# The last outer product of a two-level fast matrix product: how its held output stores are issued, and its last chunk in halves

## The chip, the cores and the metric

The kernel runs on one core of a Trainium2 chip. The metric is the device time of one execution in microseconds (us). A core has five instruction streams that matter here: TensorE (PE; its weight loads are listed apart as PEld), VectorE (DVE), ScalarE (ACT), GpSimd (POOL) and SyncE (SP). Each runs its own instructions in order, and they wait for one another through semaphores. SP and ACT can issue DMAs; before the change only SP issues the ones spoken of here.

## What is computed

An attention block feeds a two-layer block. In short, with 8 batches, 12 heads, 448 tokens and head dimension 64 (all in float32):

```python
q_n, k_n = rmsnorm(q, g_q), rmsnorm(k, g_k)
attn = softmax(q_n @ k_n.T / sqrt(64))
x = (attn @ v)            # to (8 * 448, 768)
h = x @ w_in              # w_in: 768 x 2048
out = (h - tanh(h)) @ w_out   # w_out: 2048 x 768
```

## The kernel before

The attention of later batches runs interleaved with the two layers of earlier ones. The layers are done by a seven-product scheme: a 2 x 2 block product is made of seven smaller products of sums and differences of blocks, named 1 to 7 and run in the order `ORDER = (1, 5, 6, 2, 3, 7, 4)`. The products 2, 3 and 7 accumulate into the PSUM banks of 1, 5 and 6. There are three banks for this (`mm_162`, `mm_163`, `mm_164` in the program, all "mm" in the profile).

For batches 2 to 7 the second layer is done for two batches at once, by `project_pair`, and the scheme is used twice. Outside are seven outer products in the order `OUTER = (1, 2, 3, 7, 6, 5, 4)`, whose 2 x 2 blocks are the two halves of the hidden units, the two batches, and the halves of the output columns. Each outer product makes three chunks of 128 output columns for 448 tokens (`m` = 0, 1, 2; `HC` is 3, `CD` is 6). Chunks 0 and 1 come out of seven inner products of 224 tokens, each four contractions long; the third chunk comes out of a plain product of 448 tokens and eight contractions. In the profile each float32 matmul shows as two records, so an inner product is 8 records and the third chunk 16.

After each inner product's matmuls (L1094) `flush()` runs what was put off in `late["todo"]` and one step of `late["calm"]` (two in some places of outer product 4). Then the bank is read: product 1 is copied by ScalarE to `s1` (L1168), product 2 is copied by ScalarE (L1174), the others are added by VectorE (`add`, L1101). When a chunk is whole, `combine_outer` adds it into what the pair's chunks need; the chunks that are held across outer products lie in the tiles `acc` and `acc2`. For third chunks the adds are made at once, else they go on the list `late["calm"]` as well, as do the stores.

`store(b, n, y, o)` turns a finished chunk of 128 columns by 448 tokens on VectorE in 32 x 32 blocks (L950) into another tile, and puts off the issue of its four DMAs (L955) on the list `late["out"]`. `step_out()` counts those entries down and issues them; it is called before each product's matmuls, so a store goes to SP's queue one product after its transpose stands in the program. Each of the four DMAs writes 32 partitions of 14 runs of 128 bytes to the output, 448 runs and 56 KB. All go out on SP, behind each other and behind the loads of weights into the ring `w_f` (`ring_load`), which SP issues too. Tiles that await a store are named th, th_more, s and acc.

The program is written as a fixed order per engine (`manual_schedule`): nothing is rearranged, and the order of the calls in the Python code is the order of each engine's instructions. The last outer product is number 4 for batches 6 and 7. After it, `mlp` runs the remaining `todo` and `calm` work and issues what is left in `late["out"]`. The kernel then branches over a second, general path to the closing instructions (L1797).

Of the kernel before, what the change touches and what calls it, by code (L numbers as in the profile page):

```python
# [146 lines left out]
def bounded_path(tc, ctx, q, k, v, moe_w_in, moe_w_out, out, g_col, ident, ones, half_ones, neg_half, early):  # L147
# [66 lines left out]
    def mm_bank():  # L214
        return bank_of("mm")
# [649 lines left out]
    def hidden(b):  # L865
# [74 lines left out]

        return products(b, 0, SETS, 2, HC, moving, done_with)

    def store(b, n, y, o=None):

        if o is None:
            o = part("th").rearrange("p f s -> p (f s)")
        nc.vector.transpose(out=o, in_=y if b >= FIRST else y.rearrange("r (c p) -> r p c", c=NCH))  # L950

        def issue():
            for i in range(P // BL):
                d = n * P + i * BL
                nc.sync.dma_start(  # L955
                    out=out[b * S : (b + 1) * S, d : d + BL].rearrange("(j t) d -> t j d", t=BL),
                    in_=o[i * BL : (i + 1) * BL].rearrange("t (j d) -> t j d", d=BL),
                )

        late["out"].append([1 if b >= PAIRED else 2, issue])  # L960

    def step_out(by=1):
        for entry in late["out"]:
            entry[0] -= by
        while late["out"] and late["out"][0][0] <= 0:
            late["out"].pop(0)[1]()

    def calm_step(twice=False):
        for _ in range(1 + twice):
            if late["calm"]:  # L970
                late["calm"].pop(0)()
# [93 lines left out]
    def project_pair(b, ks):  # L1065

        if ks[0] == 0:
            late["acc"] = [late["pair"].tile([P, HC, S], F32, name=name) for name in ("acc", "acc2")]
        acc, acc2 = late["acc"]
        us = late["us"]  # L1070
        low, high = slice(0, HS), slice(HS, S)
        outer_plan = {
            3: {1: (0, SETS - 1), 5: (1, SETS - 1)},
            7: {1: (2, 0), 5: (2, 1), 6: (2, 2), 2: (2, 3)},
            6: {1: (3, 0), 6: (3, 1), 3: (3, 2), 4: (3, 3)},
        }
        inner_plan = {5: 0, 6: 1, 7: 2, 4: 3}
        inner_at = {6: 0, 3: 1, 7: 2, 4: 3}
        calm = late["calm"]

        def at(k, q):

            p = OUTER[k]
            if q in outer_plan.get(p, {}):
                outer_sum(*outer_plan[p][q])
            if k == SOON and q == 1:
                inner_sum(p, 2)
                inner_sum(p, 3)
            if q in inner_at and k + 1 in ks:
                inner_sum(OUTER[k + 1], inner_at[q])  # L1090

        def matmuls(bank, n, w, moving, first):
            for i, mv in enumerate(moving):
                nc.tensor.matmul(  # L1094
                    bank[:, :n], lhsT=w(i), rhs=mv, start=(first and i == 0), stop=(i == len(moving) - 1),
                    skip_group_check=not first,
                )
                yield 4 * n / ENGINE_NS

        def add(out, x, y, op=ALU.add):  # L1100
            nc.vector.tensor_tensor(out=out, in0=x, in1=y, op=op)  # L1101

        def combine_outer(p, m, y):

            e, f = acc[:, m], acc2[:, m]
            if p in (1, 3):
                if m == HC - 1:
                    nc.scalar.copy(out=e if p == 1 else f, in_=y)
                return
            third = m == HC - 1  # L1110
            o = y
            if third and p in (2, 5, 4):
                o = f if p == 2 else e if p == 4 else part("s1").rearrange("p f s -> p (f s)")

            def soon(*args):
                if third:
                    add(*args)
                else:
                    calm.append(lambda: add(*args))

            if p == 2:
                soon(o, y, e)
                calm.append(lambda: store(b, m, o))
            elif p == 7:
                soon(e, e, y)
                soon(f, f, y, ALU.subtract)
            elif p == 6:
                soon(e, e, y)
            elif p == 5:
                soon(o, y, e)  # L1130
                calm.append(lambda: add(f, f, o))
                calm.append(lambda: store(b + 1, HC + m, o))
                calm.append(lambda: store(b + 1, m, f, o))
            else:
                soon(o, y, e)
                calm.append(lambda: store(b, HC + m, o, f if third else e))

        def flush():
            now, late["todo"] = late["todo"], []
            for fn in now:  # L1140
                fn()
            calm_step(p == 4 and q in (3, 7, 4))

        for k in ks:
            p = OUTER[k]
            step = ring_steps.index((b, 2, p, 1))
            if p in (1, 3):
                y1, y2 = ((acc if p == 1 else acc2)[:, m] for m in range(2))
            else:
                y1, y2 = (part(n).rearrange("p f s -> p (f s)") for n in ("s2", "s5"))  # L1150
            s1 = part("s1").rearrange("p f s -> p (f s)")
            banks = {}
            for i, q in enumerate(ORDER):
                ring_load(step + 5 + i // 2)
                step_out()
                w = ring_tiles[b, 2, p, 1 + i // 2][:, i % 2 * HB : (i % 2 + 1) * HB].rearrange("p (f d) -> p f d", d=P)
                first = q not in (2, 3, 7)
                bank = banks[q] = mm_bank() if first else banks[{2: 1, 3: 5, 7: 6}[q]]
                if q in (1, 2, 3):
                    moving = [rows(p, KB * (q > 1) + c, 1, high if q == 3 else low)[:, 0] for c in range(KB)]  # L1160
                else:
                    u = us.pop((p, inner_plan[q])) if q != 5 and q != 6 else us[p, inner_plan[q]]
                    moving = [u[:, c] for c in range(KB)]
                yield from matmuls(bank, HS, lambda c: w[:, c], moving, first)
                flush()
                v = bank[:, :HS]
                if q == 1:
                    nc.scalar.copy(out=s1[:, low], in_=v)  # L1168
                elif q == 5:
                    add(y2[:, low], v, s1[:, low])  # L1170
                elif q == 6:
                    add(y1[:, high], v, s1[:, low])
                elif q == 2:
                    nc.scalar.copy(out=y1[:, low], in_=v)  # L1174
                elif q == 7:
                    add(y2[:, high], v, y2[:, low])
                    add(s1[:, low], v, s1[:, low])
                elif q == 3:
                    add(y1[:, high], v, y1[:, high])
                    late["todo"].append(lambda p=p, y=y1: combine_outer(p, 0, y))  # L1180
                elif q == 4:
                    add(y2[:, low], v, s1[:, low])
                    late["todo"].append(lambda p=p, y=y2: combine_outer(p, 1, y))
                at(k, q)
            ring_load(step + 9)
            step_out()
            w = ring_tiles[b, 2, p, 0].rearrange("p (f d) -> p f d", d=P)
            bank = mm_bank()
            yield from matmuls(bank, S, lambda i: w[:, i], [rows(p, f, 1, slice(0, S))[:, 0] for f in range(HF)], True)
            flush()  # L1190
            late["todo"].append(lambda p=p, v=bank[:, :S]: combine_outer(p, HC - 1, v))

# [79 lines left out]

    def mlp():
        late["todo"], late["keep"], late["inner"], late["calm"], late["out"] = [], [], None, [], []
        for b in range(PAIRED):
            yield from hidden(b)
            yield from project(b) if b else project_first(b)
        for fn in late["todo"]:
            fn()
        late["todo"] = []  # L1280
        single_stack.close()
        late["pair"] = pool("pair", bufs=1)
        for b in range(PAIRED, B, 2):
            yield from hidden(b)
            while late["inner"] is not None:
                inner_step()
            yield from project_pair(b, range(SOON))
            yield from hidden(b + 1)
            yield from project_pair(b, range(SOON, len(OUTER)))
        for fn in late["todo"]:  # L1290
            fn()
        while late["calm"]:
            calm_step()
            step_out()
        step_out(2)
# [506 lines left out]
```

## Time and profile before

| What | Value |
|---|---|
| Median of three runs | 1356.81 us (1356.78 to 1357.18) |
| The profiled execution's own time | 1356.19 us |
| Its span, first to last instruction | 1354.4 us |
| TensorE busy | 1317.9 us, 97% of the span |
| VectorE, ScalarE, GpSimd busy | 949.1, 556.9 and 775.1 us |
| Last matmul ends | 1343.9 us |
| Last transpose on VectorE ends | 1345.2 us |
| First and last of the output stores that SP issues after 1328 us | 1328.5 and 1349.7 us |

The span is measured from the first to the last instruction on the core. The time of the execution is 1.8 us more. Times of single instructions are counted from the start of the span. A DMA's row shows how long the issuing engine was occupied with it; the landing of its data is listed apart.

### The profile page before, as it was taken

What the parts mean: (1) busy time and instruction counts of PE and PEld (TensorE: products, weight loads), DVE (VectorE), ACT (ScalarE), POOL (GpSimd) and SP (SyncE); (2) the same over time, 40 slices, a digit from 0 to 9 for tenths busy, and PEclk for the clock granted to TensorE, in tenths of its full rate; (3) what the DMA queues carried; (4) which work ended last, traced back from release to release, by engine and by line L of the source; (5) the groups of instructions that cost most, each with busy time, mean ns of one, the idle gap of its engine ahead of it and who ended that gap; (6) DMA issues with size and microseconds to landing.
All of it is one profiled execution on the core that took longest, in us unless ns stands there. A gap on an engine that the chain in (4) does not pass through costs nothing.

```text
span 1354.4 us, 29206 instructions
## 1 busy us (share of the span) xinstructions
PE 1317.9 (97%) x11336; PEld 1029.0 (76%) x11336; DVE 949.1 (70%) x1393; ACT 556.9 (41%) x1326; POOL 775.1 (57%) x591
## 2 busy tenths in 40 slices
PE   7989999999999999999999999999999999999996
PEld 3467854478998878697778787778787888699985
DVE  4999978757855768587887576768786668434453
ACT  7856654344433454445322446354512264311100
POOL 4766766347846256626698235844699253712761
PEclk9999999999999999999999999999999999999999
DMA  7879889889999667476655867476645775365544
GB/s 172 197 198 266 254 256 254 249 247 280 335 302 274 169 157 182 107 192 151 162 145 138 197 169 179 110 180 163 168 139 139 160 194 158 107 163 178 171 143 84
DMA packets 371688, 253.54 MB, mean 187 GB/s; under 512 B 282196, under 2 KB 310228, under 8 KB 371540
## 3 DMA queue, kind: packets, MB, share of 16 engines
q1 hardware_dynamic: 371536, 251.57, 68.9%
q8 instruction: 92, 1.51, 0.5%
q14 instruction: 56, 0.46, 0.1%
q10 hardware_dynamic: 4, 0.00, 0.0%
HBM read 205.23 MB, written 46.27 MB: 186 GB/s over the span
## 4 chain that ended last, share of the span: by engine, by line
PE 84%; DVE 9%; DMA 2%; SPq 2%; issue 1%; ACT 1%; POOL 1%; DVEq 0%; ACTq 0%
PE mm L841 36%; PE mm L1094 23%; PE sc L569 9%; PE sc L635 6%; PE mm L1258 5%; DVE xT L762 1%; PE sc L673 1%; PE sc L623 1%; SPq L955 1%; PE mm L673 1%; DVE rows L613 1%; DMA w_f<-w_in 1%; DVE rows L606 1%; DVE rows L600 1%; DMA w_f<-w_inner 0%
## 5 line engine op out<-in xcount | busy, mean ns | idle before, releaser
L841 PE MATMUL mm<-xT,w_f 128*128 128x224 f32 x1296 | 264.0, 353 | 0.7 <-DVE s L912 0.7
L841 PEld LDWEIGHTS mm<-xT,w_f 128*128 128x128 f32 x1296 | 244.5, 190 | 6.4 <-issue 4.8
L569 PE MATMUL sc<-qT,kT 64*32 64x448 f32 (+1 forms) x3072 | 214.2, 499 | 2.9 <-ACT p_last L575 1.7
L841 PE MATMUL mm<-tt,w_f 128*128 128x224 f32 x1044 | 213.7, 356 | 0.8 <-DMA w_f<-w_in 0.2
L841 PEld LDWEIGHTS mm<-tt,w_f 128*128 128x128 f32 x1044 | 194.9, 190 | 19.1 <-issue 15.4
L523 POOL TENSOR_TENSOR rr_mine<-rr_mine,neg_half 128x28 f32<-128x28 f32 x33 | 160.6, 4868 | 2.7
L758 DVE TENSOR_TENSOR xT<-xT,sc 128x448 f32<-128x448 f32 x32 | 19.9, 622 | 176.8 <-PE sc L569 119.3
L889 POOL TENSOR_TENSOR gT<-s,th 128x448 f32<-128x448 f32 x44 | 56.1, 1277 | 145.3 <-ACT th L888 142.0
L1094 PE MATMUL mm<-u,w_f 128*128 128x224 f32 x672 | 136.5, 354 | 1.2 <-DVE sum_all L733 0.9
L1094 PE MATMUL mm<-gT,w_f 128*128 128x224 f32 (+1 forms) x480 | 133.0, 429 | 3.1 <-DVE acc L1101 3.0
L1094 PEld LDWEIGHTS mm<-u,w_f 128*128 128x128 f32 x672 | 126.1, 190 | 8.2 <-POOL u L1051 3.9
L569 PEld LDWEIGHTS sc<-qT,kT 64*32 64x32 f32 x3072 | 71.0, 106 | 70.4 <-issue 50.5
L1094 PEld LDWEIGHTS mm<-gT,w_f 128*128 128x128 f32 x480 | 90.2, 190 | 40.7 <-issue 34.2
L635 PE MATMUL sc<-p,v_nat 64*32 64x448 f32 x1120 | 110.5, 536 | 0.0
L1094 PE MATMUL mm<-g,w_f 128*128 128x224 f32 (+1 forms) x360 | 99.5, 428 | 1.1 <-DVE acc L1101 1.1
L725 ACT COPY sum_g<-sum 32x14 f32<-32x14 f32 x280 | 56.3, 201 | 106.1 <-DVE sum L717 100.3
L889 POOL TENSOR_TENSOR g<-s,th 128x448 f32<-128x448 f32 x24 | 30.6, 1278 | 108.2 <-ACT th L888 93.3
L575 ACT ACTIVATE p<-sc 128x448 f32<-128x448 f32 x132 | 71.7, 543 | 50.3 <-PE sc L569 42.4
L1094 PEld LDWEIGHTS mm<-g,w_f 128*128 128x128 f32 x360 | 67.9, 190 | 28.2 <-issue 26.2
L1258 PE MATMUL mm<-gT,w_out 128*128 128x448 f32 x192 | 74.4, 543 | 0.0
L1051 POOL TENSOR_TENSOR u<-gT 128x448 f32<-128x448 f32 x48 | 58.8, 1247 | 11.1 <-PE mm L1094 11.1
L144 POOL TENSOR_TENSOR rr<-rr,neg_half 112x8 f32<-112x8 f32 (+1 forms) x30 | 49.4, 1675 | 26.7 <-DVE rr L143 26.2
(196 smaller groups left out, 2427.9 us busy)
## 6 DMA issues: line engine op xcount, KB each, us to landing
w_f<-w_in SPq DMA_DIRECT2D x196, 384.0 KB, 3.5
w_f<-w_inner SPq DMA_DIRECT2D x63, 512.0 KB, 3.7
w_f<-w_out SPq DMA_DIRECT2D x42, 512.0 KB, 3.9
w_raw<-in_moe_w_out_dram SPq DMA_DIRECT2D x16, 768.0 KB, 5.6
w_in<-w_out SPq DMA_DIRECT2D x21, 384.0 KB, 5.1
qk_nat<-in_q_dram SPq DMA_DIRECT2D x132, 56.0 KB, 2.8
qk_nat<-in_k_dram SPq DMA_DIRECT2D x132, 56.0 KB, 2.3
g<-w_out SPq DMA_DIRECT2D x14, 512.0 KB, 5.1
```

Source lines behind the costliest of these rows:

```text
L144: nc.gpsimd.tensor_tensor(out=r, in0=r, in1=neg_half[:rows], op=ALU.pow)
L523: nc.gpsimd.tensor_tensor(out=mine, in0=mine, in1=neg_half[:, :1].to_broadcast([P, 2 * NJ]), op=ALU.pow)
L569: nc.tensor.matmul(tiles[h][i * BL : (i + 1) * BL, :n], lhsT=kT[r, c * P + at : c * P + at + BL], rhs=qT[r, first : first + n], start=True ...
L575: nc.scalar.activation(p[:, h, c if c < 2 else 0, :], tiles[h][:, :n], AF.Exp, scale=1.0 if rr is None else rr[:, 0, 2 * c + h : 2 * c + h ...
L635: nc.tensor.matmul(av[g][i * BL : (i + 1) * BL, :S], lhsT=v_nat[keys, h, c, m * BL : (m + 1) * BL], rhs=p[keys, h], start=first, stop=True ...
L673: nc.tensor.matmul(av[n][r : r + BL, :HS], lhsT=v_nat[:, h, c, m * BL : (m + 1) * BL], rhs=p[c][:, h, n * HS : (n + 1) * HS], start=False, ...
L725: nc.scalar.copy(out=acc[h * BL : (h + 1) * BL, g], in_=part[g * BL : (g + 1) * BL, h * NJ : (h + 1) * NJ])
L841: nc.tensor.matmul(bank[:, f * HS : (f + 1) * HS], lhsT=w[:, c * width + f, :], rhs=moving[p](c), start=(first and f == 0 and c == 0), sto ...
L889: eng.tensor_tensor(out=g[:, rows, cols], in0=h, in1=th, op=ALU.subtract)
L1051: nc.gpsimd.tensor_tensor(out=u[:, half], in0=a[:, half], in1=z[:, half], op=ALU.subtract)
L1094: nc.tensor.matmul(bank[:, :n], lhsT=w(i), rhs=mv, start=(first and i == 0), stop=(i == len(moving) - 1), skip_group_check=not first,)
L1258: nc.tensor.matmul(bank[:, :S], lhsT=w_out_row(f, n // HC)[:, n % HC * P : (n % HC + 1) * P], rhs=g[:, f, :], start=(f == 0), stop=(f == C ...
```

## The change

There is a new flag, `late["ending"]`, which is set for the last outer product (number 4 of batches 6 and 7) only. With it set:

- In `flush()` all of the list `late["calm"]` is run at once, at the first inner product, and not one step at each.
- `store` issues its DMAs at once, after anything still held in `late["out"]` (`step_out(9)`), and the odd ones of the four go to ScalarE's queue and not SP's.
- Chunks 0 and 1 of this outer product's own result are added, turned and stored by the new `store_now`, two DMAs on SP and two on ScalarE.
- The third chunk is made in two halves of 224 tokens, each with its own bank, its own add, transpose and four DMAs of 32 partitions of 7 runs.

```diff
+    def store_now(b, n, y, o, cols):
+        nc.vector.transpose(out=o[:, cols], in_=y[:, cols])
+        for i in range(P // BL):
+            d = n * P + i * BL
+            (nc.sync, nc.scalar)[i % 2].dma_start(
+                out=out[b * S + cols.start : b * S + cols.stop, d : d + BL].rearrange("(j t) d -> t j d", t=BL),
+                in_=o[i * BL : (i + 1) * BL, cols].rearrange("t (j d) -> t j d", d=BL),
+            )
...
     def store(b, n, y, o=None):
...
         def issue():
             for i in range(P // BL):
                 d = n * P + i * BL
-                nc.sync.dma_start(
+                (nc.scalar if late["ending"] and i % 2 else nc.sync).dma_start(
...
+        if late["ending"]:
+            step_out(9)
+            issue()
+            return
         late["out"].append([1 if b >= PAIRED else 2, issue])
...
     def combine_outer(p, m, y):
...
+            if p == 4 and late["ending"]:
+                add(y, y, e)
+                store_now(b, HC + m, y, e, slice(0, S))
+                return
...
     def flush():
...
             calm_step(p == 4 and q in (3, 7, 4))
+            while late["ending"] and late["calm"]:
+                calm_step()

         for k in ks:
             p = OUTER[k]
+            late["ending"] = b + 2 == B and k == len(OUTER) - 1
...
             w = ring_tiles[b, 2, p, 0].rearrange("p (f d) -> p f d", d=P)
+            if late["ending"]:
+                y, o = acc[:, HC - 1], acc2[:, HC - 1]
+                for cols in (low, high):
+                    bank = mm_bank()
+                    moving = [rows(p, f, 1, cols)[:, 0] for f in range(HF)]
+                    yield from matmuls(bank, HS, lambda i: w[:, i], moving, True)
+                    flush()
+                    add(y[:, cols], bank[:, :HS], y[:, cols])
+                    store_now(b, CD - 1, y, o, cols)
+                continue
             bank = mm_bank()
```

More of the change, by code (lines that the diff above doesn't have):

```diff
@@ L1274, in mlp @@
         late["todo"], late["keep"], late["inner"], late["calm"], late["out"] = [], [], None, [], []
+        late["ending"] = False
         for b in range(PAIRED):
```

## The prediction, made before the changed kernel ran

> **What bounds the kernel now.** I read the page first, then only its last 30 us, since the diff acts nowhere else: the chain of waits by line, the end of the timeline, the tile that goes out (out_dram), and the instructions of the closing line.
>
> ```profile
> PE 1317.9 (97%) x11336; PEld 1029.0 (76%) x11336; DVE 949.1 (70%) x1393; ACT 556.9 (41%) x1326; POOL 775.1 (57%) x591
> ...
> PE 84%; DVE 9%; DMA 2%; SPq 2%; issue 1%; ACT 1%; POOL 1%; DVEq 0%; ACTq 0%
> ```
>
> TensorE is the bound up to its last matmul; after that SP's queue is (the SPq share of the chain). TensorE in the last outer product, from the timeline (columns: start, us, engine, line, op, tiles, shape, count):
>
> ```profile
> 1328.61 3.19 PE L1094 MATMUL mm<-u,w_f 128*128 128x224 f32 x16
> 1331.64 3.19 PE L1094 MATMUL mm<-gT,w_f 128*128 128x224 f32 x16
> 1334.66 3.19 PE L1094 MATMUL mm<-u,w_f 128*128 128x224 f32 x16
> 1337.69 6.18 PE L1094 MATMUL mm<-gT,w_f 128*128 128x448 f32 x16
> ...
> 1343.90 0.63 DVE L1101 TENSOR_TENSOR acc<-mm,acc 128x448 f32<-128x448 f32 x1 [4.01 <-PE mm L1094]
> 1344.57 0.65 DVE L950 STREAM_TRANSPOSE acc<-acc 128x448 f32<-128x448 f32 x1
> ```
>
> Each x16 is two inner products; product 1 ends just before the first row, the rows are 5 and 6, 2 and 3, 7 and 4, then the third chunk. It runs without a pause to 1343.87; the last data is transposed at 1345.22. SP's stores come later:
>
> ```profile
> 1347.57 0.43 SPq L955 DMA_DIRECT2D out_dram<-acc  x1
> 1349.70 0.32 SPq L955 DMA_DIRECT2D out_dram<-acc  x1
> L955 SPq DMA_DIRECT2D out_dram<-acc x12: 316/486/1073, 1342.6 to 1349.7; - x12
> DMA to landing us min/median/max: 1.7/2.7/4.0
> L1797 SPq EVENT_SEMAPHORE  x10: 17/28/28, 1353.0 to 1354.3; - x10
> ```
>
> The last chunk's four stores begin at 1347.57, 2.35 us after their data, because older stores still stand in SP's queue (0.49 us each and about 0.05 between); the last issue ends at 1350.02. SP then branches, and its closing instructions start 3.0 us later. VectorE and ScalarE show such a pause of 2.8 to 2.9 us before their closing drains too, so it isn't the wait for the last landing (1349.70 + 2.1 = 1351.8). The end is therefore the last issue's end + 4.37 = 1354.39.
>
> **Part 1: the tail gets shorter.** All older stores leave earlier and only the second half chunk is left at the end. After the last matmul: add of 224 columns 0.39 (the L1101 rows of that shape), 0.04 to the next, a transpose of 224 columns 0.41 (448 take 0.638 and 896 take 1.105 in the trace: 1.04 ns a column), 0.05 to the issue, two issues on each queue 0.32 + 0.05 + 0.48. With 0.02 at the start that is 1.76 us from the last matmul to the last issue, against 1350.02 - 1343.87 = 6.15: 4.39 less. The branch pause and closing stay; the last landing (1.28 + 2.3 = 3.6 after the last matmul, 5.3 at the longest landing shown) is hidden below the 4.8 at which closing starts, or shows by 0.5 at worst. Splitting 16 matmuls of 448 (0.376 apart) into 32 of 224 (0.189 apart) costs 0.05 us. Net of part 1: -4.3 (-3.8 to -4.4).
>
> **Part 2: ScalarE's queue gets twelve issues ahead of a copy that TensorE needs.** The diff drains all held work in the first flush of the last outer product, before product 1's copy of its bank to s1 (L1168). In the order of the changed kernel, ScalarE has twelve store issues (two of each of six tiles), then that copy. Product 2 accumulates into the same bank and waits for the copy; in the old order it had room:
>
> ```profile
> 1328.81 0.35 ACT L1168 COPY s<-mm 128x224 f32<-128x224 f32 x1 [11.67 <-PE mm L1094]
> 1333.40 0.35 ACT L1174 COPY s<-mm 128x224 f32<-128x224 f32 x1 [4.25 <-PE mm L1094]
> ```
>
> The copy ended at 1329.16, product 2 began at 1331.64. Now it must wait for the tiles' transposes, which VectorE does in one run, no longer between its bank reads. The first tile (th) is ready at 1322.3 and costs nothing. The others: A 1328.47 as now; from the present durations (adds 0.58 to 0.62, transposes 0.64, dependent ones 0.04 apart) B 1330.2, C 1330.9, D 1332.0, E 1332.7.
>
> No row shows a 448-run store issued by ScalarE; the nearest is SP's: 0.32 for the first, 0.48 + 0.05 for each after. Three limits:
> - ScalarE alone: A done 1329.4, B 1331.1, C 1332.2, D 1333.2, E 1334.2.
> - The DMA engines: in the order of either kernel an issue waits for the landing of the DMA eight before it. By the row below, 53.9% of 21.5 us for some 30 stores, a store takes 0.385 us of all 16 engines. Tile C's last lands at about 1330.25 + 1.75 + 8 x 0.385 - 0.385 = 1334.7, which E's last issue waits for: 1335.2.
> - Long issues: 6 of SP's last 32 took 0.77 to 1.45 us; of ScalarE's ten, two might, half of it under the waits: +0.5.
>
> ```profile
> q1 hardware_dynamic: 14008, 1.73, 53.9%
> ```
>
> I take 1335.7; plus 0.05, the copy's 0.35 and 0.05, product 2 starts at 1336.1: a stall of 4.5 us. From below: even with issues as short as ScalarE's shortest (0.21 us, a tiny load at the start), E at 1332.7 gives 1333.1 and a stall of 1.9, so no gain is possible here; with SP's own prices 3.0. From above: if the two queues took turns strictly, 20 issues of 0.53 from 1328.54 end at 1339.1: 7.9. Behind the copy on ScalarE is product 2's copy (follows TensorE anyway); VectorE's read of product 5 needs s1 and waits as well, and product 3 needs product 5's bank: 0.4 us after the copy, under product 2's own 1.5. Nothing else is late; ring loads for these products were issued by 1321.3.
>
> **Part 3: what the pause does to TensorE's clock.** [...] This trace has one such case (columns: window, PE, PEld, DVE, ACT, POOL, clock, DMA share, GB/s):
>
> ```profile
> 88.40:91.81 3.41, 0.87 (x5) 0.53 (x4) 3.41 (x4) 0.54 (x1) 2.46 (x3) 1.00 0.81 326
> 91.81:95.22 3.41, 3.41 (x35) 2.25 (x37) 3.34 (x5) 0.05 (x1) 1.87 (x2) 0.50 0.02 5
> ```
>
> A window three quarters idle was enough, and the next 3.41 us ran at 0.50. [...] Of a 4.5 us gap some window holds 2.54 idle us with a chance of (4.5 + 3.41 - 5.08)/3.41 = 0.83. A full cold window of work costs 1.7 us, one that begins in the gap less: I take 1.2 (0 to 1.7).
>
> **The sum:** -4.3 + 4.5 + 1.2 = +1.4 us. Span 1354.4 to 1355.8, the profiled execution's 1356.19 to 1357.6; the median of runs is 0.62 above that execution, so 1358.2. A measurement can tell about 0.2% (2.7 us) from no change: this is none.
>
> [...] with one queue the share of DMA time stays at 53.9% while SP issues nearly without a break, so issue time was the limit; at two queues the 0.385 us a store would be. That is why I don't halve the issue time in part 2.
>
> **Rivals.** (a) Copy not held up, the twelve issues finding a free ScalarE: -4.3, so 1352.5. For it: ScalarE is idle for 11.67 us before the copy. Against it: tile E doesn't exist before 1332.7 and the copy is behind it in program order. To be faster by over 0.2% the stall and the clock together must stay under 1.6 us, below the floor of 1.9; only an error in that order or in the floor allows it. Chance 0.06. (b) Slower: the two issuers take turns[...]. For it: ScalarE's first issue took 0.51 us beside one of SP's, its second 0.21. Against it: the second ran inside an SP issue that lasted only about 0.05 longer than its neighbours. Stall 7.9, clock 1.7: +5.3, so 1362.1. It decides once the last of the ten issues ends after about 1337.0 (0.85 us each): stall 5.8. Chance 0.24. (c) Likeliest: stall 3.0 to 5.8 cancels the gain: 1355.4 (stall 3.0, no clock loss, -4.4) to 1359.5. Chance 0.70.
>
> The likeliest gives 1358.2. The low end is the bottom of (c), 1355.4; upwards it takes in most of (b), 1361.8. Faster by over 0.2%: 0.06; within: 0.70; slower: 0.24.
>
> **What would show it.** A TensorE pause before product 2 of the last outer product, ended by ScalarE's copy, of 3 to 6 us; twelve DMA issues on ScalarE's queue ahead of that copy; a stretch at clock 0.50 after it; last issue under 2 us after the last matmul, with the closing line 3 us later. I'm wrong if TensorE runs through (then it is faster), if the pause is over 6 us, or if the last issue still trails by 4 us or more.

## The result and the profile after

The changed kernel is slower: 1361.82 us in the median of 11 runs (1359.8 to 1363.58), against 1357.55 us for the kernel before in 11 runs on the same chip. The ratio is 1.0030 with a 95% interval of 1.0020 to 1.0039, or +4.1 us (2.7 to 5.3). Set on the 1356.81 us from which the forecast was made, that is 1360.9 us. The forecast of 1358.2 us was 2.7 us too low; its range (up to 1361.8) holds this, with the median as timed, 1361.82, at its very edge; but its likeliest case, no change within 0.2%, did not come. The ratios here and below are formed from all runs but two slow ones (1533.58 us of the kernel before, 7848.15 us of `copy_first`), and can differ from the quotient of two medians by up to 0.0005.

The profiled execution took 1362.14 us, its span is 1360.3 us. It lies 5.9 us above the profile of before, 1.8 us more than those 4.1 us. The sum by stages below comes to 7.5 us, which is 3.4 us more. Each stage is read from one execution of either kernel, so the table shows where the time went, and its sizes are those of two single executions.

The page of the changed kernel, busy time and the chain of waits by engine:

```profile
PE 1321.3 (97%) x11352; PEld 1033.7 (76%) x11352; DVE 949.2 (70%) x1395; ACT 557.4 (41%) x1326; POOL 773.7 (57%) x591
...
PE 83%; DVE 8%; DMA 2%; SPq 2%; POOL 1%; issue 1%; ACT 1%; DVEq 0%; ACTq 0%
```

TensorE is busy 3.4 us longer with the same arithmetic. The page alone can't say whether these are dearer instructions or a slower clock. The timeline of the last outer product can (start, us, engine, line, op, tiles, shape, count, and in brackets the idle time before and what ended it):

```profile
1326.98 0.84 SPq L965 DMA_DIRECT2D out_dram<-s  x2
1326.99 0.90 ACTq L965 DMA_DIRECT2D out_dram<-s  x2
1327.05 3.19 PE L1108 MATMUL mm<-u,w_f 128*128 128x224 f32 x16
...
1333.17 1.56 ACTq L965 DMA_DIRECT2D out_dram<-s  x2
...
1334.77 0.34 ACT L1189 COPY s<-mm 128x224 f32<-128x224 f32 x1 [19.19 <-DMA out_dram<-th]
1335.17 6.30 PE L1108 MATMUL mm<-gT,w_f 128*128 128x224 f32 x16 [4.93 <-ACT s L1189]
1341.31 3.19 PE L1108 MATMUL mm<-u,w_f 128*128 128x224 f32 x16
1344.34 6.22 PE L1108 MATMUL mm<-gT,w_f 128*128 128x224 f32 x32
...
1350.59 0.39 DVE L1115 TENSOR_TENSOR acc<-mm,acc 128x224 f32<-128x224 f32 x1 [2.19 <-PE mm L1108]
1351.02 0.41 DVE L945 STREAM_TRANSPOSE acc<-acc 128x224 f32<-128x224 f32 x1
1351.45 2.39 SPq L948 DMA_DIRECT2D out_dram<-acc  x2
1351.46 2.40 ACTq L948 DMA_DIRECT2D out_dram<-acc  x2
```

Three things stand here. Product 1's copy on ScalarE, which before ran at 1328.81, comes at 1334.77, behind the twelve store issues, and TensorE's pause of 4.93 us before product 2 names that copy. The sixteen matmuls after the pause take 6.30 us where their like take 3.19. And the last two issues on each queue, forecast at 0.85 us with their gap, take 2.39 us.

TensorE's clock, from the windows (window, us, busy time of PE, PEld, DVE, ACT, POOL with counts, clock, DMA share, GB/s):

```profile
1331.06:1334.47 3.41, 0.00 (x0) 0.00 (x0) 0.00 (x1) 0.00 (x0) 0.00 (x0) 1.00 0.98 137
1334.47:1337.89 3.42, 2.72 (x7) 2.51 (x8) 0.69 (x2) 0.34 (x1) 0.00 (x0) 0.50 0.61 91
1337.89:1341.30 3.41, 3.41 (x10) 3.06 (x10) 0.00 (x0) 0.34 (x1) 0.00 (x0) 0.50 0.00 0
1341.30:1350.56 9.26, 9.25 (x49) 8.90 (x47) 4.70 (x10) 0.00 (x0) 0.00 (x0) 1.00 0.40 58
```

One window of 3.41 us is empty, and the two after it run at half clock. In the first of the two TensorE was busy for 2.72 us (80%), and the next one ran at 0.50 as well; in that one it was busy throughout, and from its end, 1341.30, the clock is 1.00 up to the last matmul. In the first row the DMA engines are 98% busy, and the chain of waits through the pause goes by the landings of stores (start, us, what):

```profile
1328.67 3.28 DMA out_dram<-th_more
1331.95 0.02 issue
1331.97 0.02 ACTq L965
1331.98 0.04 issue
1332.02 2.77 DMA out_dram<-th
1334.79 0.34 ACT s L1189
```

The stores of the last part (count; duration in ns, shortest, median and longest; first and last start):

```profile
L948 SPq DMA_DIRECT2D out_dram<-acc x8: 315/398/2032, 1343.3 to 1351.8; - x8
L948 ACTq DMA_DIRECT2D out_dram<-acc x8: 373/434/1980, 1343.3 to 1351.9; - x8
DMA to landing us min/median/max: 2.1/2.9/4.4
```

SP's part of the closing line, in the same columns, asked for in two stretches of time:

```profile
L1829 SPq EVENT_SEMAPHORE  x2: 28/28/28, 1356.7 to 1356.8; - x2
L1829 SPq EVENT_SEMAPHORE  x8: 17/28/28, 1359.0 to 1360.2; - x8
```

Before, the ten closing instructions of SP stood in one block of 1.3 us. Now two of them run, then 2.2 us pass, then the other eight.

Counted from the first store of tile A (1328.54 before, 1326.98 after; this execution came to that point 1.56 us earlier):

| Stretch | Before, us | After, us | Difference | Forecast |
|---|---|---|---|---|
| first store of A to the start of product 2 | 3.10 | 8.19 | +5.09 | +4.5 |
| start of product 2 to the last matmul's end | 12.23 | 15.38 | +3.15 | +1.25 |
| last matmul's end to the last issue's end | 6.15 | 3.30 | -2.85 | -4.39 |
| last issue's end to the end | 4.37 | 6.45 | +2.1 | 0 |
| sum | 25.85 | 33.3 | +7.5 | +1.4 |

7.5 less the 1.56 of earlier arrival is the 5.9 us between the spans. The arrival isn't part of the change: in the other kernels' profiles the first store of A starts between 1327.82 and 1331.25.

### The profile page after: what moved, and what is told of

Read it like the earlier page. It is cut to its first block, busy times and chain, and to the rows that moved or that the text cites. A ratio compares the mean times of both kernels' runs of the same rounds, so it can differ in the third digit from the quotient of the medians.

```text
span 1360.3 us, 29256 instructions
## 1 busy us (share of the span) xinstructions
PE 1321.3 (97%) x11352; PEld 1033.7 (76%) x11352; DVE 949.2 (70%) x1395; ACT 557.4 (41%) x1326; POOL 773.7 (57%) x591
## 4 chain that ended last, share of the span: by engine, by line
PE 83%; DVE 8%; DMA 2%; SPq 2%; POOL 1%; issue 1%; ACT 1%; DVEq 0%; ACTq 0%
PE mm L841 36%; PE mm L1108 23%; PE sc L569 9%; PE sc L635 5%; PE mm L1289 5%; DVE xT L762 1%; PE sc L623 1%; PE sc L673 1%; POOL u L1065 1%; DVE rows L613 1%; DMA w_raw<-in_moe_w_in_dram 1%; DVE rows L606 1%; DVE sum_T L710 1%; PE mm L673 1%; DVE rows L600 1%
## 5 line engine op out<-in xcount | busy, mean ns | idle before, releaser
L1108 PE MATMUL mm<-gT,w_f 128*128 128x224 f32 (+1 forms) x496 | 136.1, 428 | 8.2 <-ACT s L1189 4.9
L1108 PEld LDWEIGHTS mm<-gT,w_f 128*128 128x128 f32 x496 | 95.5, 195 | 43.9 <-issue 32.0
```

The costliest lines, as they stand in the source:

```text
L1108: nc.tensor.matmul(bank[:, :n], lhsT=w(i), rhs=mv, start=(first and i == 0), stop=(i == len(moving) - 1), skip_group_check=not first,)
```

## The experiments

The theory after the result: the kernel loses by one position in ScalarE's order. Product 1's copy stands behind twelve issues, this makes the pause, and the pause makes the half clock; the earlier stores and the second queue are worth about 4 us by themselves. The rivals: that two queues or the stores' density cost the time whatever the order (contention of the DMA engines), so that ScalarE must be kept out of it; that the halves cost what they save; and that part of the loss is the place where the program's code lies, which only the closing line shows.

### copy_first: the copy ahead of the drain

```diff
-                flush()
                 v = bank[:, :HS]
-                if q == 1:
+                if q == 1 and late["ending"]:
+                    nc.scalar.copy(out=s1[:, low], in_=v)
+                flush()
+                if q == 1 and not late["ending"]:
```

> The changed kernel with one instruction moved: in the last outer product ScalarE copies product 1's bank before the ten held stores that wait for data are issued, not after them. Theory Q (TensorE's 4.93 us pause is the copy standing behind the issues in ScalarE's queue, and the 6.83 us at half clock follow from the pause): the pause is gone, at most 0.5 us are left before product 4, whose bank waits for the second copy; no half clock before the last matmul; about 8 us less than the changed kernel, so 4 us faster than the kernel before, a ratio near 0.997. Theory B (the burst of two queues itself holds things up, since the DMA engines were 98% busy in the pause): a pause of 3 us or more stays before product 2 or 3, and the ratio is 1.001 or more.

Measured: 1355.1 us in 16 runs, ratio 0.9979 (0.9972 to 0.9987): faster than the kernel before, and 0.0051 (6.9 us) below the changed kernel, by the place of one copy of 0.35 us. Its timeline:

```profile
1328.18 0.35 ACT L1188 COPY s<-mm 128x224 f32<-128x224 f32 x1 [11.66 <-PE mm L1108]
...
1331.01 3.19 PE L1108 MATMUL mm<-gT,w_f 128*128 128x224 f32 x16
...
1335.58 0.34 ACT L1197 COPY s<-mm 128x224 f32<-128x224 f32 x1 [7.05 <-DMA out_dram<-th]
...
1336.02 1.75 PE L1108 MATMUL mm<-u,w_f 128*128 128x224 f32 x8 [0.31 <-issue]
...
1344.73 2.08 SPq L948 DMA_DIRECT2D out_dram<-acc  x2
```

The copy waits only for its matmuls, product 2 starts on time and at full clock. Of the twelve issues the ten that wait for data now stand behind it and ahead of product 2's copy, which comes at 1335.58. Product 4 needs that bank and starts 0.31 us late (the trace names no cause here; `copy_both` below tests it). The rival that two queues cost the time whatever the order is refuted.

### keep_clock: the pause stays, the clock is kept

```diff
+                if late["ending"] and q == 2:
+                    spare = sc_bank()
+                    for i in range(12):
+                        nc.tensor.matmul(spare[:, :HS], lhsT=w[:, i % KB], rhs=moving[i % KB], start=True, stop=True)
```

> The changed kernel with 12 more matmuls (24 records) of 224 columns into a spare PSUM bank that nobody reads, ahead of product 2 of the last outer product: work put into the pause. They take 4.6 us of the 4.9 us pause. If the half clock is caused by the pause and costs what the trace of the changed kernel says (3.1 us over products 2 to 4), this kernel does more work and is 3 us faster than the changed kernel: ratio near 1.001 against 1.003. If the half clock costs nothing of its own or comes from elsewhere, the ratio stays at 1.003 or above.

Measured: 1359.71 us in 21 runs, ratio 1.0012 (1.0005 to 1.0018), as expected: 0.0018 (2.4 us) below the changed kernel, though it does more work. The timeline, and below it the windows' row over the stage:

```profile
1333.80 4.70 PE L1188 MATMUL sc<-gT,w_f 128*128 128x224 f32 x24
1338.79 3.29 PE L1108 MATMUL mm<-gT,w_f 128*128 128x224 f32 x16 [0.29 <-ACT s L1193]
```

```profile
1330.00:1351.00 21.00, 20.71 (x109) 20.18 (x108) 10.06 (x21) 0.69 (x2) 0.00 (x0) 1.00 0.56 81
```

The extra matmuls fill the time in which TensorE waits for the copy; the clock stays at 1.00, and products 2 and 3 take 3.29 us in place of 6.30. So the half clock is a cost of its own: 3.1 us in the changed kernel's profile (half of the 6.13 us worked at 0.50) and about 2.4 by the ratios. The second figure is not the clock's alone, since the tail from the last matmul to the last issue's end is shorter here as well, 2.58 us for 3.30. Over all runs the mean granted clock is 0.9969 here and 0.9944 in the changed kernel; that is 3.4 us, of which a part falls in the idle end and costs nothing.

### held_on_sp: the held stores on SP alone

The kernel's own last chunks still go out on two queues.

```diff
-                (nc.scalar if late["ending"] and i % 2 else nc.sync).dma_start(
+                nc.sync.dma_start(
```

> The changed kernel with all stores of earlier outer products issued by SP alone, still at once and in the order of their data; the last outer product's own stores still go out by two queues. Theory Q: nothing stands ahead of the copy on ScalarE, no pause, no half clock; SP works its 20 issues off at some 0.6 us each by about 12 us after the first, which is before the last two tiles, so the end has the short tail too: ratio near 0.997. Theory B: no pause either, since there is one queue, so this run alone doesn't tell Q from B. A third theory, that the second queue is what shortens the tail, would have SP still behind at the end: last issue 4 us or more after the last matmul and ratio near 1.000.

Measured: 1358.87 us, ratio 1.0011 (1.0002 to 1.0019). The expectation was wrong. TensorE has no pause (its last matmul ends at 1343.91), yet the last issue ends at 1352.94, 9.0 us later. SP's own waits, between 1328 and 1353 us:

```profile
SPq L965 <- DMA out_dram<-acc: 8.5, 4, 4.1
```

SP stands with old stores (L965) and waits, four times and for 8.5 us together, until DMAs of acc have landed. Those are this outer product's own stores that ScalarE issued; they come later in the program than the stores that wait for them. The trace shows how: in these last 30 us the stores of both queues raise eight semaphores between them (numbers 100, 102 to 104 and 106 to 109), and a store waits for its data or for the landing of the last store that raised its semaphore. SP's store at 1338.48, with SP idle since 1334.34, waits for 107, which ScalarE's store of 1336.70 had raised; the one at 1343.82, idle since 1341.77, waits for 106, raised by ScalarE's of 1340.02. So in this trace a store awaited the landing of the DMA that held its semaphore before it, and in these waits that was a younger store on the other queue. In the traces of before and of the changed kernel, too, the stores of the end raise these eight numbers in turn. How the semaphores are dealt out when the program is built is not shown by any run.

### sp_only: all stores in the new order, on SP alone

```diff
-            (nc.sync, nc.scalar)[i % 2].dma_start(
+            nc.sync.dma_start(
...
-                (nc.scalar if late["ending"] and i % 2 else nc.sync).dma_start(
+                nc.sync.dma_start(
```

> The changed kernel with every store on SP: all at once and in the order of their data, last chunk in halves, no second queue. Each DMA has one of eight semaphores and waits for the one eight before it. Theory S (held_on_sp was slow because its semaphores are dealt out across both queues when the program is built, so that SP's stores of old tiles waited for the landing of ScalarE's stores of later ones, 8.5 us in all): with one queue that wait is gone; SP is 36 issues of some 0.55 us behind at most till 1340 and then waits for data; the last issue ends 3 us after the last matmul, and with SP's code about as long as before the closing isn't split: ratio 0.997. If one queue is simply too slow, the last issue trails by 5 us or more, and the ratio is 0.999 or more.

Measured: 1356.18 us in 13 runs, ratio 0.9996 (0.9988 to 1.0005): no difference, where 0.997 was expected. The stores of the last part, and below them the DMA queue from 1327.8 to 1349.4 us (packets, MB, share of 16 engines):

```profile
L948 SPq DMA_DIRECT2D out_dram<-acc x16: 315/468/1349, 1339.4 to 1349.0; - x16
```

```profile
q1 hardware_dynamic: 14432, 1.78, 55.3%
```

No wait for a DMA is left on SP, and TensorE has no pause. But SP issues 36 times in the 21.6 us, 0.60 us each with the gaps and the long ones, and never idle for more than 0.34 us; the last issue ends 6.2 us after the last matmul (1343.19), as it did before (6.15). The order of the stores alone buys nothing: SP's issue time is the limit. What shortens the tail is the second queue (2.99 us in `copy_first`).

### whole_chunk: the changed kernel without the halves

```diff
-                for cols in (low, high):
+                for cols in (slice(0, S),):
...
-                    yield from matmuls(bank, HS, lambda i: w[:, i], moving, True)
+                    yield from matmuls(bank, S, lambda i: w[:, i], moving, True)
...
-                    add(y[:, cols], bank[:, :HS], y[:, cols])
+                    add(y[:, cols], bank[:, :S], y[:, cols])
```

> The changed kernel without the halves: the third chunk is made by 16 records of 448 columns, one add, one transpose, two DMAs of 14 runs on each queue. By the prediction's rows the halves save 0.63 + 0.65 - 0.39 - 0.41 = 0.48 us after the last matmul and cost 0.05 on TensorE: 0.4 us slower than the changed kernel, ratio 1.0033. A rival: the smaller DMAs of the halves land earlier and this shows at the end too, 1 us or more; another: the halves cost more than they save, ratio under 1.003.

Measured: 1362.27 us in 6 runs, ratio 1.0032 (1.0021 to 1.0044), not to be told from the changed kernel's 1.0030. The pause is there again (4.61 us). The windows around its end, and below them SP's last stores:

```profile
1333.15:1336.56 3.41, 0.53 (x3) 0.53 (x4) 0.55 (x2) 0.35 (x1) 0.00 (x0) 1.00 0.99 142
1336.56:1339.97 3.41, 3.41 (x11) 3.09 (x10) 0.14 (x1) 0.35 (x1) 0.00 (x0) 0.50 0.24 36
1339.97:1350.06 10.09, 10.08 (x38) 6.76 (x36) 3.90 (x8) 0.00 (x0) 0.00 (x0) 1.00 0.33 49
```

```profile
L948 SPq DMA_DIRECT2D out_dram<-acc x2: 316/528/741, 1351.4 to 1351.8; - x2
```

Here the pause ended before the window did, the next one was busy throughout, and only one ran at half clock. The last issue takes 0.74 us and not 2.03, so that from the last matmul (1350.05) to the last issue's end it takes 2.47 us, in the changed kernel 3.30. In these two profiles the halves save 0.5 us in the add and the transpose and lose 1.3 in the last issue, and the medians show no gain: the part of the change that was to shorten the end is worth nothing here.

### after_dead: the changed kernel with its code moved

Eight DMA instructions are added to the general path over which the kernel branches. They are never executed; they only move the code behind them.

```diff
+            for _ in range(8):
+                nc.sync.dma_start(out=gcol[:, 0:1], in_=g_q[:, None])
```

> The changed kernel with eight more DMA instructions in SP's code of the general path, which is not executed: the same instructions run, and only the place of SP's closing instructions in its code shifts. Theory L (the second pause of 2.2 us inside the changed kernel's closing, after its second closing instruction, is the load of a next block of code, which the closing straddles since SP lost 16 stores): the closing now lies beyond that edge, there is one pause after the branch and none within, about 2 us less than the changed kernel, ratio near 1.0015. If the second pause is a wait for a landing or for another engine, it stays and the ratio stays at 1.003.

Measured: 1359.7 us in 13 runs, ratio 1.0019 (1.0011 to 1.0028). The closing line:

```profile
L1831 SPq EVENT_SEMAPHORE  x10: 17/28/28, 1357.4 to 1358.7; - x10
```

The ten stand in one block again, and the second pause is gone; whether a load of code had made it is not shown (see the last section). The pause before product 2 (4.7 us) and two windows at half clock are still there. The ratio falls by 0.0011 (1.5 us), but the two intervals overlap; the pairs below add to it.

### copy_first_dead, copy_first_whole and copy_first_whole_dead

`copy_first` with the same eight unexecuted instructions; with the whole third chunk, as in `whole_chunk`; and with both.

> copy_first with the same eight unexecuted DMA instructions. Theory L: copy_first's second pause of 1.9 us in the closing goes, ratio 0.9979 - 0.0014 = 0.9965. Otherwise 0.9979 again.

> copy_first with the third chunk whole (no halves). Theory F (the last issues of copy_first and of the changed kernel take 1.7 to 2.0 us and not 0.48 because a 16 KB load of TensorE's code runs at that moment, and the halves, having more TensorE instructions in its queue, put TensorE's branch, which starts that load, 3 us later against the end): without the halves the load is over before the last stores; the last issue takes under 0.8 us, the time from the last matmul to the last issue's end is 2.5 us against 3.0, so this is 0.3 to 0.6 us faster than copy_first in spite of 0.48 us more work on VectorE: ratio near 0.9976. By the prediction's rows alone it would be 0.4 us slower: 0.9982. Two runs this close may not part by time; the last issue's length decides.

> Both together with the copy first: whole chunk and eight unexecuted DMA instructions. If L and F both hold it is the fastest, near 0.996: no pause before product 2, the last issue under 0.8 us, one pause at the branch and none in the closing. If neither holds, 0.998.

| Kernel | Halves | Code moved | Median, us (runs) | Ratio (95%) | Second pause in the closing |
|---|---|---|---|---|---|
| copy_first | yes | no | 1355.1 (16) | 0.9979 (0.9972 to 0.9987) | yes |
| copy_first_dead | yes | yes | 1353.59 (6) | 0.9968 (0.9956 to 0.9980) | no |
| copy_first_whole | no | no | 1356.67 (21) | 0.9993 (0.9986 to 1.0000) | yes |
| copy_first_whole_dead | no | yes | 1353.81 (8) | 0.9974 (0.9963 to 0.9985) | no |

The first was run in another set than the other three, each beside its own runs of the kernel before. In all three pairs (with `after_dead`) the second pause vanishes with the code's place, and the ratio falls by 0.0011, 0.0011 and 0.0019; in the last pair the intervals are apart, by 0.0001. The profiles agree: from the last issue's end to the end it takes 6.42, 5.87 and 6.45 us with the code in its old place, and 4.17, 4.19 and 4.37 with it moved. With the code moved, halves and whole chunk can't be told apart.

`copy_first_whole` was slower than either expectation (0.9976 or 0.9982). Its last stores, and below them the first part of its closing line:

```profile
L948 SPq DMA_DIRECT2D out_dram<-acc x4: 316/398/624, 1343.5 to 1349.3; - x4
```

```profile
L1831 SPq EVENT_SEMAPHORE  x5: 28/28/28, 1353.3 to 1353.6; - x5
```

The last issue is short (0.62 us, where `copy_first` has 1.72), as the expectation had it, but from the last matmul to the end it takes 8.81 us, `copy_first` 8.86. The larger add and transpose cost 0.5 us, and SP's first closing instruction came 3.3 us after the branch, not 2.6. Why the ratios still differ by 0.0014 stays open; the intervals just overlap. `copy_first_whole_dead` (0.9974) is not the 0.996 that was expected, either.

### copy_both: no copy behind the drain at all

`copy_first_dead`, and product 2's copy in the last outer product goes to VectorE.

```diff
-                    nc.scalar.copy(out=y1[:, low], in_=v)
+                    (nc.vector.tensor_copy if late["ending"] else nc.scalar.copy)(out=y1[:, low], in_=v)
```

> copy_first_dead with product 2's copy of the last outer product moved from ScalarE, where it stands behind ten issues, to VectorE. In copy_first and its variants TensorE still pauses for 0.3 to 1.0 us before product 4, whose bank waits for that copy. If that is the whole of what is left of the stall, the pause goes and the ratio is 0.9968 less 0.0003 to 0.0007: 0.9963. If VectorE, now with one more bank read behind its run of transposes, becomes late itself, a pause shows before product 4 or the third chunk and the ratio is 0.997 or more.

Measured: 1352.7 us in 10 runs, ratio 0.9972 (0.9962 to 0.9981). The timeline, and below it the windows' row:

```profile
1332.09 3.19 PE L1108 MATMUL mm<-gT,w_f 128*128 128x224 f32 x16
1335.11 3.19 PE L1108 MATMUL mm<-u,w_f 128*128 128x224 f32 x16
```

```profile
1329.00:1344.30 15.30, 15.30 (x82) 15.01 (x80) 9.62 (x20) 0.34 (x1) 0.00 (x0) 1.00 0.78 111
```

TensorE has no idle time left at all in the stage. Against `copy_first_dead` (0.9968), whose profile has a gap of 0.97 us before product 4, that bought nothing that the measurement can tell. These two are the best of the kernels here, some 4 us below the kernel before.

## Why the prediction was right or wrong

**The mechanism: right.** The forecast's pause before product 2, ended by the copy behind twelve issues, is in the profile, and `copy_first` removed it by moving that copy alone. Rival (a), no pause, is refuted by the profile; what it would be worth is shown by two kernels that have no such pause and no second one in the closing: -3.2 and -2.8 in a thousand (`copy_first_dead`, `copy_both`), where (a) had computed -4.3 us, which is 3.2 in a thousand.

**The stall: right, 0.6 us too small.** 5.09 us for 4.5. VectorE was as forecast: tile E was ready at 1331.06, which is 1332.62 in the time of before, forecast 1332.7. The copy came at 1336.33 in that time, forecast 1335.7. The second of its three limits, the DMA engines, is the one that the pause shows: 98% busy, with 5431 packets in 4.93 us, which is 0.40 us of all 16 engines for a store of 448. The forecast's 0.385 came from "some 30 stores"; its row of 14008 packets is 31.3 stores, or 0.37. The third, long issues, did not come: none of ScalarE's ten took over 0.7 us.

**Rival (b), the two issuers in turn: refuted,** although its size of the loss (+5.3) is nearer than the likeliest case's. In the trace of the changed kernel the first pairs of the two queues lie over each other (SP 0.316 and 0.478 us, ScalarE 0.366 and 0.493 in the same 0.9 us). ScalarE's first issue is 0.05 us longer there than its shortest in the pause, 0.32, and not twice as long. This refutes the rival as it was priced, 0.53 us for each issue in turn; that one issuer holds the other up by some 0.05 us within an issue isn't excluded. The larger loss came from elsewhere.

**The clock: too small by more than half.** Forecast 1.2 us, measured 3.1 in the profile and about 2.4 by `keep_clock`. The step that failed is "a full cold window of work costs 1.7 us, one that begins in the gap less": it took one window as the price, from the one case in the trace of before, where TensorE was busy in all 3.41 us of the cold window (one at half clock) and no second came. That trace has no cold window that began in a pause with work behind it. In the changed kernel the first cold window was busy for 2.72 of 3.41 us, in `after_dead` for 1.27, and in both another followed:

```profile
1331.82:1335.23 3.41, 0.84 (x5) 0.49 (x3) 1.62 (x3) 0.00 (x0) 0.00 (x0) 1.00 0.91 128
1335.23:1338.64 3.41, 1.27 (x3) 1.17 (x4) 0.69 (x2) 0.34 (x1) 0.00 (x0) 0.50 0.99 145
1338.64:1342.06 3.42, 3.42 (x11) 3.08 (x10) 0.00 (x0) 0.34 (x1) 0.00 (x0) 0.50 0.02 3
```

(`after_dead`, windows.) In `whole_chunk` the pause ended before the window's edge and one was all. In these three profiles the price is half the work done in every cold window up to the first that is busy throughout, so it depends on where the pause lies against the windows: 1.7 us in `whole_chunk`, 3.1 in the changed kernel. That the clock goes by windows is read from two traces: in the changed kernel's it changed at 95.44, 1334.48, 1341.30 and 1354.96 us, with 363, 2 and 4 times 3.413 us between, in that of before at 91.82, 95.23 and 1347.92, with 1 and 367 times. The forecast's chance of 0.83, with its 2.54 idle us, was the author's estimate from one case.

**The tail: the right sign, 1.5 us too much.** 2.85 us saved for 4.39. Add and transpose took 0.39 and 0.41 us, as forecast; the failed term is the last issue on each queue, 2.03 and 1.98 us in place of 0.48. Before, long issues stood in the middle of SP's queue, and the forecast counted on them in part 2 but not at the end. Its sign "last issue under 2 us after the last matmul" therefore did not come (3.30).

**The end after the last issue: 0 forecast, +2.1 measured.** "The branch pause and closing stay" failed. The closing got a second pause, which three pairs of kernels tie to the place of the code; by the ratios it is worth 0.0011 to 0.0019 (1.5 to 2.6 us).

**The sum.** The forecast called gain and loss equal. In the profile the loss (stall and clock) was 2.5 us larger and the gain (tail and closing) 3.6 smaller, 7.5 us in the stage for 1.4; by the ratio it is 4.1 for 1.4. "Slower by over 0.2%" had been given 0.24, all for rival (b); the reasons for it were others. That the range reached far enough is luck: its upper part was there for (b), which is refuted.

**The expectations of the runs.** Two failed in the same way, `held_on_sp` and `sp_only`: both took the gain of the tail for a matter of order. It needs the second queue, and with that the copy ahead of the drain. `copy_first_whole` was slower than expected, and the gain of 0.0005 expected of `copy_both` did not show.

## What to carry to other kernels

In these runs the DMA issues on ScalarE held up what stood behind them in that engine's order, their waits included (product 1's copy came 7.5 us late): before issues are handed to a second engine, put the copies that TensorE needs ahead of them, for the same edit cost 4 us or gained 3 by the place of one copy. Price a pause of TensorE that costs it the clock with half the work of every half-clock window up to the first fully busy one, as the three profiles here had it (1.7 to 3.1 us). A tail of one or two issues has to be priced with the longest issues in the trace (2.03 us here, for a median of 0.40), and a difference of one or two us at the end of a program can be where its code lies (1.5 to 2.6 us by the three pairs): run it with a few unexecuted instructions added.

## What the runs showed of the hardware that was not expected

**The place of the code.** After its branch over the unexecuted path SP starts its first closing instruction 2.6 to 3.3 us later in every kernel here, counted from the branch's start. In five kernels, the changed one among them, a second pause of 1.7 to 2.2 us follows after two or five closing instructions; with three instructions fewer on SP it comes after five and not two, and with eight unexecuted ones added it is gone. In the changed kernel's trace loads of 8 KB of instructions (queue 14) stand in both pauses. SP's branch starts at 1353.90 and its first closing instruction at 1356.74; three such loads begin between, at 1354.80, 1354.83 and 1354.89. Two more begin at 1357.18 and 1357.29, in the second pause, 1356.85 to 1359.04:

```profile
q14 instruction: 2, 0.02, 2.8%
```

Before, two begin after the branch (1350.08), at 1350.34 and 1351.38, and one, at 1353.77, among the closing instructions with no second pause. Whose code they bring, the trace doesn't say. That the second pause is the wait for a load, at an edge between two blocks of code, was the author's theory; it agrees with these times. That a load makes these pauses was not tried by itself.

**Long issues.** Issues of 0.9 to 2.0 us, on one queue or both, stand beside a load of 16 KB of instructions (queue 8): after 1326 us there are 39 in the twelve traces, and each overlaps one. The changed kernel's DMA queues between 1351 and 1353.9 us, the time of the last issues of 2.03 and 1.98 us:

```profile
q8 instruction: 1, 0.02, 3.3%
```

In `sp_only` the three loads on that queue in the 21.6 us shown begin at 1328.33, 1340.63 and 1344.13, and SP's three issues over 1 us at 1328.70, 1340.91 and 1344.33. `whole_chunk` has no such load beside its last issues, and these take 0.74 us. In the changed kernel TensorE's closing branch starts at 1347.01, 3.5 us before its last matmul ends; with the whole chunk at 1343.52, 6.5 us before. In all twelve traces the last two of these loads start 1.0 to 1.8 and 4.5 to 5.6 us after that branch. So the halves seem to move such a load, TensorE's by these times, onto the last stores; the trace doesn't say whose code it is. That the load makes the issue long was not tried by itself; the runs show the coincidence and its absence, and no more.

**Two queues.** In the changed kernel the two queues issued side by side at nearly their own speed (0.05 us more on ScalarE) until the 16 DMA engines were full: in the pause, with these 98% busy, a store went out every 0.41 us (12.1 in 4.93 us), where SP alone in `sp_only` issued one every 0.60.
